# Modulation folded into the QKV weights, and tokens transposed by DMA instead of TensorE, in an attention and token-mixing kernel

## The chip, the cores and the metric

The kernel runs on one core of one Trainium2 chip. The metric is the time of one execution in microseconds (us) on the device. Each time below is a median of several executions, with the lowest and highest.

In the profiles PE is TensorE (PEld its weight loads), DVE VectorE, ACT ScalarE, POOL GpSimd, and SP the engine that issues the DMAs of the main queue.

## The reference, cut to what matters

One sequence of 2048 tokens of 512 features; 32 heads of 16 features; each token sees itself and the 255 before it.

```python
mod = (silu(c) @ w_mod).reshape(B, 6, 1, -1)
sa, ca, ga, sb, cb, gb = ...                     # shift, scale, gate; twice
h = layernorm(x) * (1 + ca) + sa                 # the modulation in question
x = x + ga * attention(h, wqkv, wo)              # softmax over a window of 256
h = layernorm(x) * (1 + cb) + sb
x = x + gb * token_mlp(h, w1, b1, w2, b2)        # gelu, products over the tokens, F = 1792
```

`sa` and `ca` are one vector each, the same for all tokens. So `h @ wqkv` equals `layernorm(x) @ ((1 + ca) * wqkv) + sa @ wqkv`: the scale can go into the rows of the weights, and the shift becomes a bias.

## The kernel before

The tokens go through in four groups (G = 0 to 3) of four tiles of 128. For each group, x is normalised (`xn`), transposed so that features lie on the partitions (`h1T`), and multiplied by the weights to give Q, K and V. Attention then runs in 75 chunks: S on TensorE (scores into PSUM), one large exp on ScalarE (`et<-psa`, about 1.45 us, and a smaller one for `psb`), and AV on TensorE. Groups 1 to 3 are projected while earlier chunks run: group 1 is needed by chunk 10 or 11, group 2 by about 30, group 3 by about 41. After the exp of the last chunk come 81.6 us, the last 66 of them mostly matmuls.

In groups 1 to 3 of the kernel before, TensorE transposes, and VectorE applies scale and shift as it copies the result out of PSUM:

```python
te.transpose(pt[:, i, tile], xn[tl][:, dc * P : (dc + 1) * P], identity[:])     # 16 a group
ve.tensor_scalar(out=h1T[:, dc, cols], in0=pt[:, i, :],                          # 4 a group
                 scalar1=modFM[:, 4 + dc : 5 + dc], scalar2=modFM[:, dc : dc + 1],
                 op0=ALU.mult, op1=ALU.add)
... # group 0 has a special first half (h1p) with the scale alone, and a Q/K bias for it
te.matmul(pq, lhsT=wqkv[:, dc, c0 : c0 + P], rhs=h1T[:, dc, cols], start=dc == 0, stop=dc == 3)
```

There is one `h1T`, so group G can be written into it only when the last projection of group G-1 has read it.

Every step is an op with a number, and the program is emitted in the order of one long list, which a search has tuned. The instructions of each engine are emitted in the order of its part of the list:

```python
def run_order(ops):
    for word in ORDER.split():            # about 1380 numbers; a letter picks the engine
        o = ops[int(word.rstrip("ADP"))]
        ...                               # error if something it depends on is not out yet
        o.emit(...)
```

The softmax here doesn't subtract the row's maximum and nothing guards it: scores larger than these inputs give would overflow.

## Time and profile before

| | kernel before |
|---|---|
| time | 267.24 us (267.21 to 267.5) |
| span of the profile | 264.8 us |
| first exp | 17.38 us |
| exp of chunk 10, 30, 41, 50, 74 | 42.45, 87.20, 111.06, 130.11, 183.23 us |
| from the exp of chunk 74 to the end | 81.57 us |
| TensorE clock | 1.00 everywhere |

### The profile page before, as it was taken

The page shows a single profiled execution, that of the slowest core. Times are in us where ns is not written, and L with a number is a line of the kernel's source. Part 1 is how long each engine was busy: PE and PEld are TensorE (multiplying, and loading weights), DVE is VectorE, ACT ScalarE, POOL GpSimd, SP SyncE. Part 2 cuts the span into 40 slices and gives each one's busy share as a digit, 9 for nine tenths or more (in the row PEclk, how much of TensorE's full clock was granted, in tenths as well). Part 3 has the DMA queues.
Part 4 walks back from the last instruction along what each step waited for, and adds up shares of the span by engine and source line. Part 5 has one row for each costly group of instructions (what it writes and reads, how often), then busy time and mean ns, then how long its engine had stood idle before and what let it go on. Part 6 is the DMA issues. An engine that isn't in the chain of part 4 may idle for free.

```text
span 264.8 us, 10695 instructions
## 1 busy us (share of the span) xinstructions
PE 248.2 (94%) x4769; PEld 136.8 (52%) x4769; DVE 193.5 (73%) x435; ACT 185.4 (70%) x268; POOL 95.9 (36%) x182
## 2 busy tenths in 40 slices
PE   7898999999998988899999999999999999999993
PEld 2576667656556654455544454445444444444441
DVE  5778896777847359999948888999998730415875
ACT  3479999999999899999999999999416431000000
POOL 8755321495289945553893031440000000000000
PEclk9999999999999999999999999999999999999999
DMA  7995400000017000000014862020499800001122
GB/s 212 369 382 197 42 5 6 2 5 2 2 49 196 5 4 5 2 2 2 5 38 128 227 172 85 2 61 23 152 362 397 360 2 0 21 0 63 59 99 79
DMA packets 31599, 25.35 MB, mean 96 GB/s; under 512 B 6076, under 2 KB 29632, under 8 KB 31552
## 3 DMA queue, kind: packets, MB, share of 16 engines
q1 hardware_dynamic: 31544, 24.66, 29.5%
q8 instruction: 37, 0.61, 0.9%
q14 instruction: 10, 0.08, 0.1%
q10 hardware_dynamic: 8, 0.00, 0.0%
HBM read 22.55 MB, written 2.10 MB: 93 GB/s over the span
## 4 chain that ended last, share of the span: by engine, by line
PE 67%; ACT 19%; DVE 8%; issue 4%; POOL 0%; ACTq 0%; POOLq 0%
PE pu L194 32%; ACT et L194 15%; PE pxy L194 13%; PE psa L194 8%; PE pq L194 5%; PE pa L194 4%; PE pv L194 3%; ACT lz L194 3%; DVE st L194 2%; DVE VT L194 1%; PE pt L194 1%; DVE part L194 1%; DVE OT L194 1%; PE psb L194 1%; DVE h L194 1%
## 5 line engine op out<-in xcount | busy, mean ns | idle before, releaser
L194 ACT ACTIVATE et<-psa 128x1536 bf16<-128x1536 f32 x75 | 109.1, 1455 | 4.0 <-PE psa L194 2.1
L194 PE MATMUL pu<-hb,w1p 128*128 128x512 bf16 x224 | 53.1, 380 | 0.8 <-DVE part L194 0.8
L194 PE MATMUL pu<-guT,w 128*128 128x512 bf16 x224 | 49.0, 379 | 0.0
L194 ACT ACTIVATE et<-psb 128x512 bf16<-128x512 f32 x75 | 45.1, 601 | 0.0
L194 PE MATMUL pxy<-et,ones_bd 128*32 128x192 bf16 (+3 forms) x960 | 38.7, 233 | 0.9 <-issue 0.9
L194 PE MATMUL pxy<-et,VT 128*32 128x192 bf16 (+3 forms) x960 | 38.4, 234 | 0.9 <-DVE OT L194 0.5
L194 PEld LDWEIGHTS <-w 128*128 128x128 bf16 x224 | 21.9, 98 | 26.4
L194 PE MATMUL psa<-QT,KT 32*128 32x192 bf16 (+3 forms) x720 | 29.8, 230 | 5.6 <-ACT et L194 4.9
L194 PEld LDWEIGHTS <-w1p 128*128 128x128 bf16 x224 | 20.3, 98 | 25.5 <-issue 2.3
L194 POOL TENSOR_SCALAR KT<-kb,mask_par 128x512 bf16<-128x512 bf16 (+1 forms) x36 | 22.9, 645 | 25.9 <-DVE kb L194 22.2
L194 PE MATMUL pq<-h1T,wqkv 128*128 128x512 bf16 (+1 forms) x128 | 30.1, 355 | 0.3 <-ACT VT L194 0.3
L194 PEld LDWEIGHTS <-KT 32*128 32x128 bf16 x960 | 16.1, 92 | 26.2 <-issue 23.9
L194 PEld LDWEIGHTS <-VT 128*32 128x32 bf16 x960 | 23.6, 96 | 11.6 <-issue 10.1
L194 PE MATMUL psb<-QT,KT 32*128 32x192 bf16 (+3 forms) x240 | 29.3, 231 | 0.0
L194 DVE SCALAR_TENSOR_TENSOR o<-pu,b2FM,bc_all 128x512 f32<-128x512 f32 x16 | 11.6, 748 | 20.2 <-PE pu L194 20.0
L194 DVE TENSOR_TENSOR et<-et,maskt 128x512 bf16<-128x512 bf16 (+2 forms) x56 | 24.9, 480 | 0.6 <-ACT et L194 0.5
L194 PEld LDWEIGHTS <-ones_bd 128*32 128x32 bf16 x960 | 23.2, 97 | 1.2 <-issue 1.1
L194 DVE BATCH_NORM_STATS2 st<-x 128x6 f32<-128x512 bf16 x32 | 21.7, 680 | 1.3 <-DMA x<-in_A_x_dram 1.1
L194 DVE TENSOR_TENSOR OT<-pxy,lz 128x256 bf16<-128x256 f32 x32 | 13.4, 420 | 10.6 <-ACT lz L194 10.1
L194 PEld LDWEIGHTS <-wqkv 128*128 128x128 bf16 x192 | 14.0, 97 | 13.4 <-issue 4.8
L194 PE MATMUL pv<-wqkv,h1T 128*32 128x256 bf16 x512 | 17.9, 274 | 0.2 <-DVE VT L194 0.2
L194 PE MATMUL pa<-wod,OT 128*128 128x512 bf16 x64 | 17.3, 381 | 0.3 <-ACT part L194 0.3
(113 smaller groups left out, 358.2 us busy)
## 6 DMA issues: line engine op xcount, KB each, us to landing
w1p<-in_B_w_dram SPq DMA_DIRECT2D x14, 512.0 KB, 6.1
w<-in_B_w_dram SPq DMA_DIRECT2D x14, 512.0 KB, 8.4
wmod<-in_w_mod_dram SPq DMA_DIRECT2D x6, 512.0 KB, 5.5
x<-in_A_x_dram SPq DMA_DIRECT2D x16, 128.0 KB, 4.8
out_dram<-otile SPq DMA_DIRECT2D x16, 128.0 KB, 1.7
wqkv<-in_A_wqkv_dram SPq DMA_DIRECT2D x2, 384.0 KB, 5.4
wqkv<-in_A_wqkv_dram SPq DMA_DIRECT2D x1, 512.0 KB, 5.0
wod<-in_A_wo_dram SPq DMA_DIRECT2D x1, 512.0 KB, 8.4
```

The costliest lines, as they stand in the source:

```text
L194: ins = call(*args, **kwargs)
```

## The change

The intent: take 48 transposes off TensorE and 12 passes off VectorE, and let the DMA queue, nearly idle at that time (DMA share 0.02 from 36 to 66 us of the kernel before), do it. The transpose in the diff takes no scale and no shift, so the modulation has to be done elsewhere: in the weights and in biases.

```diff
+# scale: rows of wqkv times (1 + ca); first heads' Q and K into a new tile wqs, the rest in place
+ve.tensor_scalar(out=dst, in0=wqkv_cols[k], scalar1=modFM[:, 4 + k : 5 + k], scalar2=0.0, ...)
+# shift: V bias by 32 narrow matmuls, copied once to SBUF
+te.matmul(ps_vb[...], lhsT=sa_rep[:, part, k, :], rhs=wv[:, k, q // 2, :, :], ...)
 # groups 1 to 3
-te.transpose(...)                                      # 16 a group
-ve.tensor_scalar(out=h1T[...], in0=pt, scalar1, scalar2, ...)   # 4 a group
+sp.dma_start_transpose(out=h1T[:, :, i * P : (i + 1) * P], in_=xn[i][:])    # 4 a group
 # Q and K leave PSUM
-ve.tensor_copy(out=QT, in_=pq)            # bias only in the first half of group 0
+ve.tensor_scalar_add(out=QT, in0=pq, scalar1=qkb)
 # V leaves PSUM
-copy(e, VT_or_vn, pv)                     # two halves of group 0 on ScalarE
+ve.tensor_tensor(out=VT_or_vn, in0=pv, in1=vb, op=ALU.add)      # VectorE alone
-xn = wpool.tile(..., bufs=5)
+xn = wpool.tile(..., bufs=4)
-ORDER = """43 3 0 4 41 ..."""
+ORDER = """44 3 0 4 31 ..."""             # searched anew, all of it
```

## The prediction

> **What bounds the kernel now.** I read the page's table of busy time first, then a cut of the execution into stretches, then the chain of work that ended last, then the groups of instructions. The table says who is full over all (columns: busy us, share of the span, instructions):
>
> ```profile
> span 264.8 us, 10695 instructions
> PE 248.2 (94%) x4769; PEld 136.8 (52%) x4769; DVE 193.5 (73%) x435; ACT 185.4 (70%) x268; POOL 95.9 (36%) x182
> ```
>
> PE leads at 94%, but that is an average over stages. The cut shows the stages (columns: stretch, its length, then busy us and count of each engine, the clock, the DMA share, GB/s):
>
> ```profile
> 17.40:36.00 18.60, 16.47 (x508) 11.98 (x500) 15.14 (x37) 17.33 (x26) 9.47 (x26) 1.00 0.52 136
> 36.00:66.00 30.00, 29.62 (x912) 19.08 (x908) 22.07 (x48) 28.52 (x37) 13.93 (x22) 1.00 0.02 4
> ...
> 76.00:123.60 47.60, 41.98 (x1192) 25.68 (x1194) 36.04 (x83) 46.43 (x62) 32.10 (x43) 1.00 0.14 36
> 123.60:154.00 30.40, 30.40 (x690) 15.95 (x687) 23.87 (x52) 29.61 (x41) 14.61 (x19) 1.00 0.39 103
> 154.00:189.00 35.00, 34.44 (x712) 17.78 (x711) 32.21 (x80) 32.89 (x52) 9.17 (x11) 1.00 0.20 54
> 189.00:199.00 10.00, 9.08 (x42) 3.92 (x41) 9.67 (x22) 2.41 (x9) 0.00 (x0) 1.00 0.97 347
> 199.00:264.80 65.80, 61.46 (x284) 27.69 (x283) 34.36 (x54) 10.59 (x16) 0.00 (x0) 1.00 0.28 106
> ```
>
> There are four kinds of time. Up to 17.4 us: a start with short dependent steps. From 17.4 to 189: attention in 75 chunks, where PE and ACT are both nearly full; ACT is idle for only 7.3 us of 171.6 (this cut with the 66 to 76 stretch included: 164.34 busy) and PE for 8.9, of which 5.6 lie in 76 to 123.6. So that middle is ACT's (46.43 of 47.60), and 36 to 76 and 123.6 to 189 are PE's with ACT 1 to 2 us behind. From 189 to 199: a DVE chain (9.67 of 10.00). From 199: matmuls alone, 284 in 61.46 us, 0.216 us each.
>
> The transposes in question, in the groups (count, busy us and mean ns, idle before) and in the chain (start, length):
>
> ```profile
> L194 PE MATMUL pt<-identity,xn 128*128 128x128 bf16 x56 | 4.1, 219 | 0.1
> L194 DVE TENSOR_SCALAR h1T<-pt,modFM 128x512 bf16<-128x512 bf16 x12 | 5.9, 535 | 0.9 <-PE pt L194 0.9
> L194 DVE CAST kb<-pq 128x512 bf16<-128x512 f32 x12 | 8.2, 682 | 1.6 <-PE pq L194 1.4
> 36.14 1.00 PE pt L194 x16
> 67.50 0.57 PE pt L194 x8
> 68.09 1.00 DVE h1T L194 x2
> 70.31 1.04 POOL rs L194
> 71.36 1.46 ACT et L194
> ```
>
> Group 1's transposes cost 1.00 us of chain, group 2's 0.45 (65.16) and 0.57, followed by 1.00 of h1T on DVE; group 3's, at 104.8, lie in ACT's stretch and are not on the chain at all.
>
> [...] a record lasts 219 ns and, pipelined, 16 took 1.00 us, 0.0625 us each[...] 128 KB here land in 1.7 us at best (the output stores), 4.8 in a busy queue[...].
>
> **The change, part by part.** The order of all instructions was laid anew, so I compared the orders of the two built programs engine by engine and priced the differences with rows of the trace.
>
> PE. 48 transposes go (64 to 16): 48 x 0.0625 = 3.0 us. The V bias adds 32 narrow matmuls of 256 columns; 64 such took 1.89 us of chain (PE pv at 17.17), so 0.95 us. Nothing else changes in count.
>
> DVE. Out: 12 h1T of 512 columns, 12 x 0.535 = 6.4 us, and 4 smaller, 1.6. In: the bias makes 24 casts of Q and K into tensor-scalar operations. With 256 columns the bias form took 477 ns (QT with qkb) against 410, so I charge 0.065 each: 1.6. V changes from cast to addition; additions from PSUM of this size run 684 (part), as the cast does (688): nothing. Two V halves come over from ACT (1.4), six weight scalings (about 2.3 by the 408 ns of an SBUF pass of 512), four multiplications or additions of h from POOL (1.7), two xn and two hb (1.7), two memsets (1.0), a vb and a sa_rep copy (0.7), a merged h1T copy (0.7). Out of DVE: four small nm (0.7). Sum: -8.0 - 0.7 + 11.1 = +2.4, spread. POOL loses about 8 us; it bounds nothing.
>
> ACT. In attention it loses two V halves and one h1T (0.59 + 0.59 + 0.57) and gains a QT and a kb of 256 columns (2 x 0.47) and one part copy (0.6): -0.2 us. So the stretch that ACT bounds hardly shortens.
>
> The start. In the kernel before, S of chunk 0 begins at 16.62 and the first exp at 17.38. In the new order DVE has the statistics of x2 and x3 ahead of modFM. x3 is issued at 4.92 and lands 4.5 us later, at 9.4; after its 0.68 and 0.18 modFM is ready at about 10.4, against 8.1 before. Behind that lie three small copies, xn x2 (0.8), the bias, h1T; on ACT two h1T of 512 (0.6 each), then two wqs (0.48 each, like h1p), then two larger scalings (1.5 together), then the first QT. I get wqs complete at 14.8, QT of the first block at 16.7, and since the two PSUM buffers of Q and K come free only then, the second block at about 17.5, S of chunk 0 near 17.8, the first exp near 18.4: +1.0 us. Against this the new order puts chunk 0 after 16 instead of 32 Q/K matmuls, so 16 of them (0.135 each, 12 took 1.62: 2.2 us) follow later.
>
> PE work from S of chunk 0 to the last output projection: 56 transposes fewer (-3.5), 16 small Q/K more (+2.2): -1.3 us. By stretches of chunks, with AV at 0.019 (64 in 1.22) and pa, pu and pq512 at 0.216: chunks 0 to 22 lose 40 transposes, 8 pa, 32 pv, 4 pq512 and gain the 16 small ones, -3.9; chunks 23 to 49 +0.8; chunks 50 to 73 gain 128 AV and 16 pv and lose 4 pu, +2.0; the rest -0.3. So work moves from the first PE-bound part into the last. In the first, ACT's idle can give back at most 3.2 us (1.27 + 1.48 + 0.44 from 17.4 to 76), of which I take 1.5. In the last, PE was full (64.84 of 65.4), so 2.0 us more cost about 1.5.
>
> The end. After the last pa both orders hold 96 + 224 matmuls: the same 69 us. The DVE chain before it has three part additions in between instead of five (-1.2 us on DVE), but PE has as much to fill the time with: 0.
>
> Sum, with the 0.2 of ACT: +1.0 - 1.5 + 1.5 - 0.3 - 0.2 = +0.5. The order was however searched for this kernel, and the pieces that I rounded (group 2's chain at 65 to 71, 2.0 us of transposes and h1T with a DVE that then runs freer) speak for some gain more; I take 1.1 for that. Net: -0.6, 267.2 to 266.6.
>
> **Rivals.** (a) The transposes by DMA come late. In group 1 all four must wait until the last Q/K of group 0 has read h1T, and the first Q of group 1 needs all four. Between these PE has 96 AV and 76 S, some 4 us of PE work, and three chunks of exp, about 6.5 us at 2.24 a chunk (74 steps in 165.85 us). [...] Groups 2 and 3 have more room (five chunks and four). For it: no trace shows such a DMA. Against: the queue is empty at 36 to 76 (share 0.02). (b) The transposes were the bound of both PE-bound parts and ACT follows: then 3.0 us go in full with the chain of group 2, giving 263. Against: ACT's few idle us. (c) The start weighs more than I think, or the weight scalings collide with the first K and Q evictions: another 1 to 2 us, 268.5. For: [...] both have the scalings ahead of the first evictions. (d) The weight loads for the later product share the queue with group 3's transposes; if they wait, group 3 starts late by a chunk, +2. The order puts only two loads ahead of them.
>
> **Range and chances.** Small terms of both signs that mostly cancel give 266.6; 264.0 if (b) holds mostly, 270.0 if (a) is moderate or (c) full. A change over 2% is 5.3 us: faster would need nearly all of ACT's idle, 0.04; slower needs a bad (a), 0.07; the rest 0.89.
>
> **What would show it.** First exp near 18.4 (start term). The exp of chunk 50 near 129 (130.11 before), ahead in spite of the later start, and that of chunk 74 about level with 183.23 (the shift of work). pt at 16 instructions, h1T on DVE gone after 40 us, kb with bias near 745 ns, vn near 690. The landing of a DMA transpose near 2 to 3 us, and no wait of PE's pq for it in groups 1 to 3. A last stretch of about 61.5 us after the hb. Wrong would be: PE idle for more than 1 us in front of pq for a DMA; a first exp before 17; an attention end earlier by over 2 us.

## More of the kernel before

Beside each execution stands the mean clock that the hardware granted to TensorE, as a share of full speed.

The starts of the exps are the ruler of this document: 75 marks that every version has, so that time lost or won can be placed between two of them. The lines of the profile that carry the reading stand in the prediction. Three rows that it doesn't show are needed later: TensorE's busy tenths in 40 slices, its granted clock in the same slices, and the shares of the chain that ended last.

```profile
PE   7898999999998988899999999999999999999993
...
PEclk9999999999999999999999999999999999999999
...
PE 67%; ACT 19%; DVE 8%; issue 4%; POOL 0%; ACTq 0%; POOLq 0%
```

The kernel before takes 267.1 to 268.0 us in all groups of runs.

## The result

The changed kernel takes 279.18 us (276.27 to 281.57, four runs) beside 267.37 us for the kernel before on the same chip: 4.05% slower. The 95% interval of the ratio is 1.0317 to 1.0493. A ratio here is the mean time of one kernel's fast runs over that of the other's in the same rounds, so it isn't quite the ratio of the medians. Executions over 1.5% slower than the fastest of the same kernel are left out of the means. One of the four runs, 281.57 us, counts as slow. The prediction of 266.6 us, with a range of 264 to 270, is wrong.

The runs of the changed kernel scatter much more than those before, and their granted clocks scatter with them: the fast runs took 276.27, 278.33 and 280.03 us at 0.988, 0.981 and 0.969. In the profiled one, (1 - 0.981) x 276.6 = 5.3 us of full-speed TensorE time are missing.

The page of the changed kernel:

```profile
span 276.6 us, 10703 instructions
...
PE 251.9 (91%) x4753; PEld 137.2 (50%) x4753; DVE 196.8 (71%) x436; ACT 185.1 (67%) x265; POOL 89.4 (32%) x178
...
PE   8699965998999798689889999999999999999993
...
PEclk9869999999999799999999999999999999999999
...
PE 57%; DVE 19%; ACT 10%; DMA 5%; issue 5%; SPq 1%; POOL 1%; DVEq 0%; ACTq 0%; POOLq 0%
```

TensorE has holes where it had none (6 in slices 2, 6 and 17, 5 in slice 7), the clock falls in slices 2, 3 and 14, and of the 19 points of the chain that PE and ACT lost, DVE and DMA have taken 16. The cut at the exps of chunks 0, 10, 30, 40 and 50 shows where the time went (columns: stretch, its length, busy us and count of PE, PEld, DVE, ACT and POOL, clock, DMA share, GB/s). Before:

```profile
0.00:17.38 17.38, 14.94 (x169) 8.55 (x173) 12.78 (x50) 8.04 (x19) 11.88 (x55) 1.00 0.95 313
17.38:42.45 25.07, 22.94 (x721) 16.69 (x710) 20.16 (x47) 23.32 (x34) 10.19 (x27) 1.00 0.39 102
...
87.20:108.95 21.75, 18.41 (x546) 11.45 (x545) 15.73 (x36) 21.62 (x30) 14.35 (x23) 1.00 0.02 4
108.95:130.11 21.16, 20.36 (x545) 12.03 (x544) 20.17 (x48) 21.14 (x29) 10.73 (x13) 1.00 0.02 4
```

After, the same chunks:

```profile
0.00:20.33 20.33, 16.64 (x183) 9.59 (x184) 13.40 (x51) 7.77 (x16) 10.66 (x53) 0.83 0.97 295
20.33:45.67 25.34, 20.70 (x644) 14.74 (x642) 19.43 (x43) 22.73 (x34) 8.32 (x16) 1.00 0.47 100
...
90.89:115.69 24.80, 21.10 (x552) 12.57 (x548) 18.97 (x43) 21.37 (x29) 15.76 (x24) 0.93 0.21 45
115.69:139.74 24.05, 19.89 (x488) 10.98 (x489) 21.01 (x50) 21.03 (x29) 6.53 (x9) 1.00 0.37 91
```

The start grew by 2.95 us at a clock of 0.83, chunks 30 to 40 by 3.05 at 0.93, chunks 40 to 50 by 2.89 at full clock. The chain of the changed kernel gives the places (start us, length, what):

```profile
3.83 4.88 DMA x<-in_A_x_dram
8.74 0.71 DVE st L193
9.65 0.59 DVE st L193
...
14.54 1.83 PE ps_vb L193 x24
16.37 1.83 PE pq L193 x8
...
43.55 3.09 DMA h1T<-xn
46.77 1.02 PE pq L193 x4
...
91.05 1.79 issue
92.84 1.77 PE pxy L193 x50
...
111.51 0.57 SPq L193
112.17 5.78 DMA h1T<-xn
118.09 1.02 PE pq L193 x4
```

- **Start.** The statistics of x2 and x3 stand ahead of modFM on VectorE, as predicted. TensorE idles from 8.58 to 10.54. After that, eight small Q/K matmuls take 1.83 us, 0.229 each; the chain before has twelve in 1.62, 0.135 each.
- **Group 1.** The first Q waits for the fourth DMA transpose until 46.64.
- **Chunk 30 to 31.** TensorE stands for 1.79 us with no wait that the profile shows ("issue"). Then 50 AV matmuls take 1.77 us, 0.035 each, where 64 took 1.22 (0.019 each) at full clock.
- **Group 3.** The fourth transpose is issued behind a weight load and takes 5.78 us.

How far each exp is behind the kernel before, in the profiles (us; the other columns are experiments, told below):

| exp of chunk | changed | e0 | e5 | e6 | s3 | b3 | b2 |
|---|---|---|---|---|---|---|---|
| 0 | 2.95 | 1.27 | 2.30 | 1.41 | 2.02 | 0.33 | 0.19 |
| 6 | 0.92 | -0.76 | 0.26 | 0.21 | -0.01 | 0.32 | 0.20 |
| 7 | 2.72 | 0.46 | 1.16 | 1.56 | 0.87 | 0.32 | 0.20 |
| 9 | 2.78 | 0.52 | 1.42 | 1.61 | 0.92 | 0.33 | 5.11 |
| 11 | 4.54 | 2.84 | 2.75 | 2.03 | 2.38 | 0.33 | 5.91 |
| 30 | 3.69 | 1.75 | 2.24 | 1.36 | 1.37 | 4.38 | 11.21 |
| 31 | 7.10 | 3.84 | 2.29 | 1.41 | 1.40 | 4.38 | 11.21 |
| 40 | 6.74 | 3.92 | 2.24 | 1.50 | 1.85 | 4.38 | 11.34 |
| 41 | 9.21 | 7.12 | 3.50 | 1.48 | 1.83 | 4.38 | 13.25 |
| 50 | 9.63 | 8.08 | 3.93 | 1.91 | 2.26 | 4.38 | 13.65 |
| 74 | 12.79 | 11.25 | 7.12 | 5.10 | 5.32 | 4.37 | 14.15 |
| end | 11.8 | 10.2 | 6.1 | 4.1 | 4.5 | 4.4 | 14.2 |

The first column read from step to step: +2.95, -2.03 by chunk 6, +1.80 to chunk 7, +0.06 to 9, +1.76 to 11, -0.85 to 30, **+3.41 to 31**, -0.36 to 40, **+2.47 to 41**, +3.58 to 74, and about -1.0 in the tail.

### The profile page after: what moved, and what is told of

Same layout as the page of the kernel before. It is cut to its first block, busy times and chain, and to the rows that moved or that the text cites.

```text
span 276.6 us, 10703 instructions
## 1 busy us (share of the span) xinstructions
PE 251.9 (91%) x4753; PEld 137.2 (50%) x4753; DVE 196.8 (71%) x436; ACT 185.1 (67%) x265; POOL 89.4 (32%) x178
## 4 chain that ended last, share of the span: by engine, by line
PE 57%; DVE 19%; ACT 10%; DMA 5%; issue 5%; SPq 1%; POOL 1%; DVEq 0%; ACTq 0%; POOLq 0%
PE pu L193 30%; PE pxy L193 9%; ACT et L193 8%; PE pq L193 6%; PE psa L193 6%; DMA h1T<-xn 3%; DVE st L193 3%; PE pa L193 2%; DVE et L193 2%; PE pv L193 2%; DMA x<-in_A_x_dram 2%; ACT lz L193 2%; DVE h L193 2%; DVE kb L193 2%; DVE part L193 1%
## 5 line engine op out<-in xcount | busy, mean ns | idle before, releaser
L193 PE MATMUL pxy<-et,VT 128*32 128x192 bf16 (+3 forms) x960 | 39.1, 236 | 3.6 <-issue 1.8
L193 POOL TENSOR_SCALAR KT<-kb,mask_par 128x512 bf16<-128x512 bf16 (+1 forms) x36 | 24.0, 678 | 32.6 <-DVE kb L193 27.4
L193 PEld LDWEIGHTS <-VT 128*32 128x32 bf16 x960 | 24.7, 97 | 14.7 <-issue 13.1
L193 PE MATMUL pq<-h1T,wqkv 128*128 128x512 bf16 (+1 forms) x120 | 25.9, 338 | 3.0 <-DMA h1T<-xn 2.5
L193 PEld LDWEIGHTS <-ones_bd 128*32 128x32 bf16 x960 | 24.0, 98 | 2.0 <-issue 2.0
L193 PE MATMUL pv<-wqkv,h1T 128*32 128x256 bf16 x512 | 18.7, 278 | 1.4 <-issue 1.4
L193 POOL TENSOR_SCALAR VT<-vn,half_m 128x512 bf16<-128x512 bf16 x24 | 17.6, 742 | 6.8 <-DVE vn L193 6.8
```

Source lines behind the costliest of these rows:

```text
L193: ins = call(*args, **kwargs)
```

## The experiments

Seventeen kernels ran in five groups; all passed the comparison with the reference. Three of them (e6, b2, b3) leave out or swap data; the comparison's tolerance didn't notice, and only their times are used. Each stands beside the kernel before in its own group. Medians and ranges are of all runs, ratios of the fast ones alone; the first group, e4 and e9 have one slow run each.

| run | us: median (range) | ratio to before, 95% interval |
|---|---|---|
| changed, first | 279.18 (276.27 to 281.57) | 1.0405 (1.0317 to 1.0493) |
| e0_control | 276.36 (275.49 to 276.93) | 1.0343 (1.0319 to 1.0368) |
| e1_start_order | 281.38 (280.27 to 281.82) | 1.0498 (1.0473 to 1.0524) |
| e2_keep_warm | 275.24 (273.62 to 276.41) | 1.0271 (1.0230 to 1.0313) |
| e3_tensor_transposes | 280.20 (278.95 to 281.80) | 1.0467 (1.0417 to 1.0516) |
| e4_queue_order | 275.39 (273.76 to 279.47) | 1.0261 (1.0221 to 1.0301) |
| e5_warm_queue | 272.75 (272.29 to 273.06) | 1.0210 (1.0193 to 1.0227) |
| e6_unread_transposes | 270.38 (270.11 to 272.02) | 1.0135 (1.0103 to 1.0167) |
| e7_tensor_early | 277.84 (277.25 to 279.01) | 1.0407 (1.0379 to 1.0435) |
| b2_dma_in_before | 278.05 (276.65 to 280.71) | 1.0399 (1.0339 to 1.0460) |
| e9_first_heads_first | 277.08 (276.49 to 280.97) | 1.0344 (1.0318 to 1.0370) |
| e10_two_buffers | 286.08 (284.77 to 286.98) | 1.0691 (1.0645 to 1.0736) |
| e11_all | 289.60 (289.43 to 291.80) | 1.0838 (1.0796 to 1.0880) |
| s1_loads_later | 275.51 (274.18 to 276.17) | 1.0306 (1.0270 to 1.0342) |
| s2_pairs | 272.14 (270.12 to 273.15) | 1.0175 (1.0118 to 1.0232) |
| s3_pairs_loads | 269.91 (269.45 to 270.99) | 1.0109 (1.0079 to 1.0138) |
| b3_free_in_before | 270.37 (268.37 to 270.91) | 1.0097 (1.0058 to 1.0135) |
| b4_spread_loads | 267.55 (267.02 to 268.36) | 0.9992 (0.9980 to 1.0003) |

In the diffs, lines with "order" show places in the list by the names of the ops.

### e1_start_order: the order of the start

```diff
-order: fm ... st(x2) fm st(x3) modFM rs(x2,x3) tr(x0,x1) nm qkb-matmuls ... wqs qkb-copy ... sa_rep
+order: fm ... fm modFM tr(x0,x1) qkb-matmuls wqs qkb-copy sa_rep st(x2) st(x3) rs(x2,x3) nm ...
```

> Changed kernel with one edit: in the start, the modulation vectors, the Q/K bias copy, the hi/lo copy for the V bias and the four scaled weight blocks of the first heads come before the statistics of token tiles 2 and 3 on VectorE and ScalarE; nothing else moves. Theory A (the order of the start is what lost it: VectorE waited for x2 and x3, TensorE stood 1.96 us and then ran at about half clock): no wait for modFM above 0.5 us, the clock digits of slices 2 and 3 at 9, the first exp at about 17.2 us instead of 20.33, the time about 3 us below the changed kernel's 279.2, so near 276. Rival B (the new bias and weight scaling work is itself too long): the first exp stays at or above 19.3 and the time within 1 us of 279.

Measured: 281.38 us, first exp 21.45, clock digits 8 and 6 in slices 2 and 3 as before the edit. Theory A fell, in the form that I gave it. The wait for modFM went, but the first Q and K still stood behind the transposes of x2 and x3 on TensorE, so the gap only moved: TensorE now idled 2.61 us, from 11.03 to 13.64, for xn of x2 and x3. Exchanging two parts of a serial chain didn't shorten it here. Rival B isn't shown either, since the gap and half clock (12.2 to 19.1 us) are in the 21.45 as well.

### e2_keep_warm: the gap filled, the waits kept

```diff
-order: fm warm fm tr(x0,x1)            # warm: one dummy matmul of 512 columns
+order: fm fm warm x9 tr(x0,x1)
```

> Changed kernel with one edit: nine more dummy matmuls of 512 columns (0.213 us each) on TensorE in the gap of 1.96 us before the second transposes, everything else in its old order, so every wait for data stays. Theory A2 (the gap itself makes the clock fall, and the fall is more than half of the 2.95 us that the first exp is late): clock digits of slices 2 and 3 at 9, vb 24 matmuls in about 0.9 instead of 1.83 us, pq 8 in about 1.1 instead of 1.83, first exp at 18.4 to 18.9, time near 277.5. Rival B2 (data waits alone): first exp stays at 20.0 or later and time near 279; also if the clock falls for another reason it still shows 8 and 6.

Measured: 275.24 us, ratio 1.0271 against 1.0405 and 1.0343 of the two groups of the changed kernel. First exp 19.21, a little above what was expected, and by chunk 5 it was level with the kernel before (+0.03 us). The clock in the two kernels over the same 6.9 us, the changed kernel first, with its stretch after the stall at chunk 30 as well:

```profile
11.40:18.30 6.90, 6.81 (x81) 4.43 (x78) 4.38 (x16) 3.06 (x7) 3.67 (x16) 0.51 1.11 347
...
92.84:98.00 5.16, 5.16 (x125) 3.61 (x125) 1.50 (x5) 2.47 (x4) 1.65 (x4) 0.67 0.02 6
```

```profile
11.40:18.30 6.90, 5.88 (x95) 4.13 (x96) 6.00 (x22) 4.29 (x9) 3.62 (x16) 1.00 1.10 344
```

Half clock (0.51) against full clock (1.00): work that does nothing, put into the gap, kept the clock up in this profile and made the kernel faster. That part of theory A2 holds. Its other part holds too. x3 landed 0.87 us later in this profile than in the first, so the first exps don't compare directly; from modFM (ready at 10.56 and 11.42 us) to the first exp it took 9.77 us in the changed kernel and 7.79 in e2. The fall cost about 2.0 of the 2.95 us. Some of the gain in time lies elsewhere, since chunk 30 to 31 took 2.15 us in this profile instead of 5.51.

### e0_control: the changed kernel once more

> The changed kernel itself once more, as the control of this group of runs on one chip. All theories: 276 to 282 us, mean granted clock between 0.96 and 0.99, first exp near 20.3. If the clock drops sit at the same places as in its first profile (11 to 18 us and 91 to 97 us), they belong to the order of the work; if they move from run to run, they depend on how the gaps fall in time.

Measured: 276.36 us, in another group of runs. The first exp came at 18.65 in this profile and the start had full clock; the clock now fell from 41.1 to 44.5 and from 116.2 to 119.6 us instead. So the places of the drops aren't fixed by the order of the work. A plain pair for it: TensorE waits 1.57 us for ScalarE ahead of chunk 9's scores in the first profile of the changed kernel (40.95 to 42.51) and in e3 (39.39 to 40.96). In the first, full speed followed (clock 1.00 from 42.10 to 45.52); in e3, half clock (0.50 from 41.23 to 44.64). And in s1 (below), a gap of 2.58 us (112.31 to 114.89) was followed by full clock.

The traces show what the drops have in common. Each drop to half clock lasts 3.41 us or twice that, and within one trace the drops start whole multiples of 3.41 us apart: 11.38 and 93.31 in the changed kernel are 24 apart. So I cut each of the 14 fast profiles with a drop into windows on its own grid. Ahead of all 22 drops, TensorE had been idle for at least 1.77 us of the window just before. Of the 1046 windows at full clock that no drop followed, two had that much (1.80 in e0, 1.88 in s1). The wait of 1.57 us is an example. In e3 all of it lies in one window, which idles 3.41 - 1.51 = 1.90 us in sum, and the next runs at half clock. In the changed kernel it falls into two, the first of which idles 1.49. First e3, then the changed kernel:

```profile
37.82:41.23 3.41, 1.51 (x76) 1.19 (x78) 1.11 (x4) 3.41 (x6) 0.00 (x0) 1.00 0.00 0
41.23:44.64 3.41, 3.22 (x94) 2.87 (x84) 2.00 (x4) 2.36 (x4) 0.00 (x0) 0.50 0.02 5
```

```profile
38.69:42.10 3.41, 1.92 (x74) 1.28 (x65) 1.74 (x5) 3.20 (x4) 0.00 (x0) 1.00 0.31 44
42.10:45.52 3.42, 2.31 (x112) 2.07 (x111) 2.60 (x6) 3.40 (x7) 0.00 (x0) 1.00 0.70 118
```

So the length of a single gap doesn't tell: gaps of 1.57 us (e3) and 1.96 us (changed kernel) were followed by half clock, and one of 2.58 us (s1) wasn't. The sum over a window of the grid tells more, with at least 1.77 us ahead of all 22 drops. The grid doesn't begin with the execution: the drops at 11.38 us in the first profile of the changed kernel and at 41.1 us in e0, the same kernel, are 8.7 times 3.41 us apart. That fits drops that move from run to run with the work unchanged.

### e3_tensor_transposes and e7_tensor_early: the DMA transposes undone

```diff
-sp.dma_start_transpose(out=h1T[:, :, i * P : (i + 1) * P], in_=xn[i][:])   # 4 a group
+te.transpose(pt[...], xn[tl][...], identity[:])                           # 16 a group
+ve.tensor_copy(out=h1T[:, dc, :], in_=pt[:, j, :])                         # 4 a group
 order e3: all of a group just ahead of its first projection
 order e7: in two halves, earlier; with the edits of e2, and group 3's xn early as in e4
```

> Changed kernel with the 12 DMA transposes of groups 1 to 3 undone: 48 TensorE transposes and 12 plain VectorE copies instead, each group's placed behind the AV work that stands just before its first projection; weights and biases as changed. Theory A3 (the DMA transposes lose 1.3 us in group 1 and 2.5 in group 3, partly because they wait in the queue, more than the 3 us of TensorE work that they save where TensorE is not the bound): time 2 to 4 us below 279.2, so 275 to 277; chunk 10 to 11 takes 2.3 us instead of 3.44, chunk 40 to 41 at most 2.9 instead of 4.58. Rival B3 (they are hidden and the loss is elsewhere): the time goes up by 1 to 3 us, since TensorE and VectorE take the work back. If the two cancel, within 1 us.

> The same kernel as e5_warm_queue with the transposes of groups 1 to 3 on TensorE and 12 plain VectorE copies, now placed better than in e3: group 1's first half in the 1.57 us in which TensorE waits for ScalarE before chunk 9's scores, the second half behind these scores, groups 2 and 3 also in two halves. Theory (four DMA transposes in a row, 1.2 us or more each in the queue and 2.4 to 3 to land, are slower than 1 us of TensorE and 1.5 of copies): 1 to 2.5 us below e5_warm_queue, chunk 10 to 11 at most 2.4 us. Rival (TensorE has no room for 3 us more): equal or up to 2 us above.

Measured: 280.20 us for e3 and 277.84 for e7, which is 5.1 us above e5 in the same group. Both theories fell: undoing the part that looked guilty gained nothing. The ratio of e3 lies above that of e0 in another group, and not clearly above that of the first group. In e3, TensorE waited 0.85 us between the two halves for the copies in group 1, and again in group 3. In e7, chunk 10 to 11 took 2.10 us, as hoped, but chunks 9 to 10, 25 to 27 and 39 to 40 lost it again. In both, the queue no longer waited for transposes, so four weight loads went out together around 85 to 93 us, and TensorE's stall there grew to 2.15 and 1.99 us. The order was searched for DMA transposes; that its loads, evictions and PSUM buffers fit no other is likely and not shown. So these two runs don't say that TensorE transposes are bad; they say that putting them back into this order, in these two places, lost.

### e4_queue_order: the last transpose ahead of the loads

```diff
-order: xn2 hb touch w1p-load touch hb hb xn3 ... transpose3    # group 3; GpSimd and the queue
+order: xn2 xn3 transpose3 hb touch w1p-load touch hb hb
```

> Changed kernel with one edit: the fourth normalised tile and the fourth DMA transpose of group 3 stand before two hb, two small copies and a 512 KB weight load on GpSimd and the DMA queue, instead of behind them. Theory A4 (the transpose was issued late and landed in 5.78 us because a weight load was in front of it): it lands in 2.4 to 3.2 us, the first Q of group 3 no longer waits for a DMA by more than 0.5 us, chunk 40 to 41 takes about 2.3 to 2.6 us instead of 4.58, time about 2 us lower, near 277. Rival B4 (a transpose is slow by itself, whatever is in the queue): landing stays above 4 us and the time within 0.7 us of 279.2.

Measured: 275.39 us. Chunk 40 to 41 took 3.31 us instead of 4.58, and TensorE's waits for transposes summed to 2.7 us (4.1 in the first profile of the changed kernel, 3.8 in e0). The longest landing was 4.2 us. The direction of A4 holds; a rest of 1.2 us stayed. The other weight loads start right behind the fourth transpose; that they cause the rest isn't shown. The fast runs of e4 span 273.76 us at clock 1.000 to 276.02 at 0.987, so its gain in time isn't this step alone.

### e5_warm_queue: both together

The edits of e2 and e4.

> Changed kernel with both edits of the runs before: nine dummy matmuls in the gap of the start, and the fourth transpose of group 3 ahead of hb, small copies and weight load. Theory: the losses are separate terms, so what stays over the kernel before is group 1's wait for its transposes (1.5), the late VectorE at chunk 7 (0.7), a rest of group 3 (1.2) and the work moved behind chunk 41 (2.6), about 6: 273 to 274, clock 0.99 to 1.00 and fewer differences between runs. Rival (both runs won the same 3 to 4 us, because both happened to miss the clock drop at 91 us): 275 to 276.

Measured: 272.75 us, 273 to 274 expected; clock 0.991 to 1.000, and a range of only 0.8 us. It is 5.65 us above the kernel before, where e0 in the same group is 9.26 above it and the first group 11.81: four tenths to half of the loss is gone with nothing done to the arithmetic. The rival's figure, 275 to 276, is out.

### e6_unread_transposes: nobody waits for the DMA

```diff
-rhs=h1T[:, dc, cols]
+rhs=h1T[:, dc, cols] if G == 0 else xres[4 * G + dc][:]      # wrong on purpose; V likewise
```

> The same kernel as e5_warm_queue, wrong on purpose: the projections of groups 1 to 3 read tiles of x instead of h1T, so the 12 DMA transposes still run and nothing waits for them. Theory: the wait for them is worth group 1's 1.5 us and group 3's 1.2 us: about 2.5 us below e5_warm_queue, no wait of pq for a DMA. Rival (another wait, of VectorE or ScalarE, ends at about the same time): less than 1 us below.

Measured: 270.38 us, 2.37 below e5 in the same group, as expected (2.5). TensorE's waits list for e5 has this line (us, times, longest), and e6's list has none for a DMA:

```profile
PE pq L193 <- DMA h1T<-xn: 1.6, 2, 1.2
```

So in the mended order the waits for the transposes are worth 2.4 us, with what follows from them: the profile of e5 has one clock drop of 3.41 us, that of e6 none. Even with free transposes and nearly full clock (0.99 to 1.00), the changed kernel stays 1.35% behind. The e6 column says where: chunk 6 to 7 (+1.35), and chunk 50 to 74 (+3.19, with about 1.0 back in the tail).

### e9_first_heads_first, e10_two_buffers, e11_all: three attempts that lost

```diff
 e9: order: ... modFM tr(x0,x1) qkb-matmuls wqs K0 Q0 evictions, then st, xn, tr of x2 and x3   (+ e4)
 e10:
-h1T = wpool.tile([P, ND, D], BF, name="h1T"); E_BUFS = 6
+h1Ts = [wpool.tile([P, ND, D], BF, name=f"h1T{n}") for n in range(2)]; E_BUFS = 5
 order e10: xn and transposes of groups 1 and 3 earlier                                        (+ e5)
 run_order e10: a number waits in the list until what it depends on is out, instead of an error
 e11: e9 and e10, without the dummies of e2
```

> Changed kernel with the queue edit of e4 and another order of the start: the first K and Q, which need only x0 and x1, on TensorE ahead of the transposes of x2 and x3, with their weight blocks, bias and evictions ahead of the statistics of x2 and x3; no added dummy matmuls. Theory (the serial chain x2, x3, modFM, then all Q/K is what makes the start late): no gap above 1 us, first exp at 16.5 to 17.5, chunk 5 about 1 to 1.5 us earlier than in e5_warm_queue, time 271 to 272. Rival (the exps of chunks 1 to 7 wait for other Q/K and V work anyway): chunk 7 within 0.5 us of e5_warm_queue and time 272.3 to 273.

> e5_warm_queue with two h1T buffers instead of one (paid for with 5 instead of 6 exp tiles), and the normalised tiles and DMA transposes of groups 1 and 3 issued earlier, which a second buffer allows. Theory (the wait for the transposes comes from the single h1T, which lets the first of them start only behind the last projection of the group before, with some 5.7 us left for four in a row): no wait of pq for a DMA above 0.3 us, time near the 270.4 of e6_unread_transposes, so 270 to 271. Rival (five exp tiles hold back ScalarE, or VectorE gets later elsewhere): 272.5 or more.

> Both edits together: first heads first in the start, two h1T buffers with early transposes, and the queue edit. Theory (separate terms): the sum of what the two runs gain over e5_warm_queue, so 268.5 to 270, still 1.5 to 3 us above the kernel before, because the added VectorE work and the work moved behind chunk 41 stay. Rival (one hides the other): no better than the better of the two by more than 0.3 us.

Measured: 277.08, 286.08 and 289.60 us. e9: its fast runs, 276.49 to 277.42, are no better than e4's (273.76 to 276.02), and the theory of the start isn't supported. e10 removed the wait for the DMA entirely, but lost far more elsewhere. TensorE's waits in e5 and in e10, and a wait of ScalarE in e10 that e5's list doesn't have:

```profile
PE psa L193 <- ACT et L193: 5.3, 16, 1.6
```

```profile
PE psa L194 <- ACT et L194: 19.4, 31, 1.8
...
ACT et L194 <- PE pxy L194: 16.7, 17, 2.0
```

The last line is exps that wait, 17 times, for AV matmuls to have read an exp tile: the price of five tiles instead of six. As a test of the second buffer the run is spoilt by this price, and what a second `h1T` alone would give is open, since no run has it beside six exp tiles. e11, with both edits, lost most.

### b2_dma_in_before: the DMA transposes alone, in the old order

```diff
 # kernel before
+            if G:
+                sp.dma_start_transpose(out=h1T[:, :, i * P : (i + 1) * P], in_=xn[i][:])
-            16 TensorE transposes and 4 VectorE passes a group        # wrong on purpose: no modulation
```

> The kernel before with one part of the change alone: groups 1 to 3 transposed by 12 DMAs, each issued right behind its normalised tile, in the old order of everything else; wrong on purpose, since these groups are then not modulated. 48 TensorE transposes (3.0 us) and 12 VectorE passes (6.4 us) go. Theory (in a row of four the DMAs land too late: first issue after the last projection of the group before, 1.2 to 1.3 us each in the queue, 2.4 to 3 us for the last): the first pq of group 1 waits some 3 to 4 us, groups 2 and 3 together 0 to 3, some of it given back, time 268.5 to 272. Rival (as predicted, they fit and the transposes' TensorE time is gained): 265 to 267.

Measured: 278.05 us, worse than either theory. Group 1 cost 5.72 us from chunk 8 to 11 (in the old order its first projection comes only about 4 us after the last of group 0): TensorE waited 3.34 us for the transposes, and the clock was half from 40.2 to 47.0. Group 3 cost 1.91 us. Another 4 us went from chunk 28 to 30, where TensorE stood for 2.70 us without a visible wait and then ran slow. In this profile half clock covers 20.5 us in all, three drops of 6.83. So this one part of the change, put into the old order, loses as much as the whole change in its own, the clock included.

### b3_free_in_before: the same with nobody waiting

b2 with the projections of groups 1 to 3 reading tiles of x, as in e6: the DMA transposes run, TensorE and VectorE are relieved, nothing waits.

> The kernel before, wrong on purpose: the 12 DMA transposes run as in b2 and the 48 TensorE transposes and 12 VectorE passes are gone, but the projections of groups 1 to 3 read tiles of x, so nothing waits for a transpose. Theory (the prediction's premise: work taken off TensorE and VectorE is worth 1 to 3 us in this order, if only nothing waits): 264.8 to 266.8. Rival (the removed work stood beside ScalarE's exps and gives nothing, or the weight loads now issued later bring a stall as in b2): 267.3 or more, and a stall near chunk 28.

Measured: 270.37 us. The kernel before and b3, from the exp of chunk 0 to that of chunk 28:

```profile
17.38:82.13 64.75, 61.51 (x1883) 40.63 (x1874) 47.98 (x106) 61.53 (x83) 33.67 (x62) 1.00 0.23 59
```

```profile
17.71:82.46 64.75, 58.70 (x1841) 38.88 (x1843) 44.23 (x98) 61.52 (x84) 33.67 (x62) 1.00 0.32 75
```

TensorE has 2.8 us and VectorE 3.7 us less to do, and the stretch takes 64.75 us in both. From chunk 30 to 74 the distance stays at 4.38 or 4.37 as well. **The removed work was worth nothing in this order, even free.** The exps follow each other at the same pace; ScalarE is busy for 61.5 of the 64.75 us in both. The new order says much the same: in e6, from chunk 0 to 22, the distance goes from 1.41 to 1.53 us with free transposes. What b3 loses is one event between chunks 28 and 29, with half clock for 3.41 us behind it (in brackets what the idle time ahead is put down to):

```profile
86.56 2.11 PE L194 MATMUL pv<-wqkv,x 128*32 128x256 bf16 x35 [3.62 <-issue]
```

### s1_loads_later: the stall at chunk 30

```diff
-order: ... w1p-load w1p-load (near chunk 28) ... five w1p-loads (behind group 3)
+order: ... five w1p-loads, w1p-load w1p-load (all behind group 3)
```

> Changed kernel with one edit: the first two 512 KB loads for the later product, issued near chunk 28, stand behind the other five of their kind, after group 3's transposes. Theory (the loads make TensorE's stall at chunk 30 to 31, for example by holding up its instructions): no issue stall above 0.9 us there, chunk 30 to 31 at most 2.8 us instead of 5.5 and 4.2 in the two profiles of the changed kernel, time 2 to 3 us below 276.4 to 279.2, so 274 to 276.5. Rival (the stall belongs to the place in the program): a stall of at least 1.2 us at the same matmuls, time as the changed kernel.

Measured: the stall is gone. Chunk 30 to 31 in the changed kernel, and in s1:

```profile
90.89:96.40 5.51, 3.72 (x109) 3.04 (x106) 3.01 (x8) 2.32 (x3) 3.41 (x6) 0.72 0.02 4
```

```profile
90.63:92.76 2.13, 2.13 (x109) 1.84 (x102) 2.10 (x6) 2.13 (x3) 1.93 (x4) 1.00 0.05 12
```

The same 109 matmuls take 2.13 us instead of 5.51. In time the gain is less clear (275.51 us; ratio 1.0306, its interval overlaps that of e0), and the clock of its four runs is 0.975 to 0.988: in the profiled one it fell from 41.4 to 48.2 us instead.

Which mechanism? The DMA view lists a queue `q8 instruction`, with 37 packets in the whole profile of the changed kernel. One of them lies in the quarter of a microsecond from 90.25, at the very end of the two weight loads:

```profile
q8 instruction: 1, 0.02, 29.4%
```

TensorE resumes at 92.84, 2.3 to 2.6 us later. In e0, such a packet comes from 88.25 and TensorE resumes at 90.91; in e3 94.25 and 97.09; in b2 89.25 and 92.18; in b3 83.75 and 86.56; in the kernel before 83.50 and 86.16. In s1, without the loads, packets lie near 87.25 and 91.0 and there is no stall. So TensorE resumes 2.3 to 2.9 us after a packet that came late, behind the weight loads. That the loads make the stall is shown by s1; that instructions arrive late is argued from these times, for the profile doesn't name the engine that a packet is for. In the changed kernel 6.7 us lie between this packet and the one before it, where 3.5 to 5 are usual; in the kernel before, the packet isn't late by that measure.

### s2_pairs and s3_pairs_loads: half as many transposes

```diff
-h1T = wpool.tile([P, ND, D]);     4 x sp.dma_start_transpose(out=h1T[:, :, i * P : (i + 1) * P], in_=xn[i])
+h1T = wpool.tile([P, 4, ND, P]);  2 x sp.dma_start_transpose(out=h1T[:, i - 1 : i + 1], in_=xn_pair)
 s2: with e5's edits; s3: with e5's and s1's
```

> e5_warm_queue with two tiles to one DMA transpose, so 6 issues instead of 12; h1T laid out by tile for it. Theory (the row of issues at 1.2 us each is what is late): the second transpose of group 1 has landed at least 1.2 us earlier after the last projection of group 0, the waits of pq for a DMA fall from 1.6 to below 0.7 us, time 0.7 to 1.5 us below 272.75. Rival (a transpose of twice the size takes twice the time to issue or land): issue near 2.4 us or landing above 4.5, waits and time as e5_warm_queue or worse.

> s2_pairs with the loads moved as in s1. e5_warm_queue had a stall of only 0.7 us at chunk 30 to 31, so the theory of the loads expects 0.3 to 0.8 us less than s2_pairs, about 271; rival: no difference within 0.3 us, or slower if the late loads arrive late for the product.

The transposes of the changed kernel, then of s2 (issue time ns as lowest/median/highest, first and last start; then the time from issue to landing):

```profile
L193 SPq DMA_TRANSPOSE h1T<-xn x12: 1188/1215/2545, 38.2 to 112.2; - x12
...
DMA to landing us min/median/max: 2.4/2.9/5.8
```

```profile
L193 SPq DMA_TRANSPOSE h1T<-xn x6: 1233/1260/1505, 37.0 to 107.2; - x6
...
DMA to landing us min/median/max: 3.1/3.2/3.4
```

Two tiles cost one issue of 1.26 us and land in 3.2 us: the issue hardly grows, and the landing by 0.3 to 0.6 (2.9 in the changed kernel, 2.6 in e5). All waits of pq for a DMA vanished. s2 took 272.14 us, 0.6 below e5's median but not clearly (it ran in another group, and its runs scatter from 270.12 to 273.15). Chunk 40 to 41 takes 2.09 us, and s2 still had the stall, 1.35 us. s3 without it: 269.91 us, the best changed version, 1.1% behind the kernel before. Its gain over s2, 2.2 us, is larger than the 0.3 to 0.8 expected, but the intervals of the two ratios overlap. The stall of s2 is longer than the 0.7 us that the expectation took from e5; the mean clock of both is 0.993. The rest isn't explained.

### b4_spread_loads: is the stall worth something before?

```diff
-order: three w1p-loads together at chunk 25
+order: one there, one behind chunk 31's scores, one behind chunk 40's
```

> The kernel before with one edit: of the three 512 KB weight loads that it issues together at 76.89 us, one stays, one goes behind chunk 31's scores and one behind chunk 40's. Theory (instruction packets wait behind loads): no issue stall above 0.3 us at chunk 29 to 30, which takes 2.2 us instead of 2.93, time 0.5 to 0.9 us below the kernel before, so about 266.4 to 266.8. Rival (ScalarE's exps have the slack to hide 0.9 us there): within 0.2 us of the kernel before.

Measured: 267.55 us, ratio 0.9992 (0.9980 to 1.0003): the same. The one stall of 0.87 us became three, of 0.28, 0.43 and 0.33 us, and from the exp of chunk 10 to that of chunk 50 it took 88.07 us, where the kernel before takes 87.66. The rival's figure holds. No version that ran beats the kernel before.

## Why the prediction was wrong

**The gain had no place to go.** The prediction credited the removed PE work with 1.5 us in chunks 0 to 22 ("In the first, ACT's idle can give back at most 3.2 us", of which it took 1.5), and 1.1 more, mainly for group 2. This step failed. b3 measures it in the old order: 0.00 us, with the work gone and nothing to wait for. In the new order, with free transposes (e6), the distance from the kernel before grows by 0.12 us from chunk 0 to 22 instead of falling by 1.5. A PE row of 8 and 9 in nearly every slice, and an ACT that idles now and then, didn't mean that less PE work lets ACT start earlier.

**Rival (a) was right in a mild form, 1.6 us of waiting in group 1, and my sum against it was wrong.** The sum put the four landings below the 6.5 us of three chunks of exp; the landing times in it were my estimate, and no run had shown them. The four transposes of group 1 took 8.4 us in the changed kernel, from 38.24, right behind the last projection of group 0, to 46.64. Four landings of the median 2.9 us would make 11.6 one after the other, so they overlap and weren't the term: each transpose holds the queue for 1.2 us (the first even 2.54), and the last then needs 3.09. Group 3 had room, but a weight load and GpSimd's order in front, rival (d), which I had named with 2 us and not taken into the sum; it was 2.47. The waits of both groups: 4.1 us as delivered, and 2.4 us of time even in the mended order (e5 to e6).

**Two things were missing from the sum.** The first is the clock. Every row of the profile before reads 1.00, and I priced each step at that rate. The change opened gaps in TensorE, and TensorE came back at half speed: 0.51 for 6.9 us of the start, 0.67 for 5 us behind the stall. The predicted first exp, 18.4, is about what the changed kernel does when the clock holds (18.65 in e0, 18.58 in s1); in the first profile it was 20.33, though modFM was ready at 10.56 us, near the 10.4 predicted. So "+1.0 us" at the start was sound as a sum of steps (+1.27 measured), and it costs nothing in the end, since e0 is 0.76 us ahead by chunk 6. The second is TensorE's stall behind the weight loads. The kernel before has it too, 0.87 us, and there its split into three smaller ones left the time the same (b4, ratio 0.9992). In the new order it was 1.8 us, with a clock drop behind it in one profile: +3.41 and +2.09 us.

**What was right.** The shift of PE work into the last part was priced at +1.5 us with 0 for the end; measured from chunk 50 to 74 +3.16, tail about -1.0, together +2.1. The count of 128 more AV matmuls there was right (704 against 580 before by the trace: 124), and the tail gave a part back, which I hadn't counted. The bias form of V was free, as said; the changed kernel's group line has 687 ns, the cast before 688:

```profile
L193 DVE TENSOR_TENSOR vn<-pv,vb 128x512 bf16<-128x512 f32 x12 | 8.2, 687 | 4.9 <-PE pv L193 4.9
```

The landing (median 2.9 us) lay in the expected 2 to 3. The sign "no wait of PE's pq for it in groups 1 to 3" was wrong: 4.1 us in two waits.

**What stays open.** Chunk 6 to 7, +0.7 to +1.8 us in all fast profiles of the new order: TensorE stands 0.5 to 1.4 us in front of some of group 0's last V matmuls, without a visible wait, while VectorE, alone with all V evictions, is late. No run separates the two. The other half of the change, the modulation in weights and biases, was never run alone, so its own cost isn't known. For the clock, windows with 1.77 to 1.88 us of idle time went both ways, and why some drops last twice 3.41 us isn't settled. The gains of the mends don't simply add up to the loss, since the mean clock changes with them as well (0.969 to 0.988 in the fast runs of the changed kernel, 0.991 to 1.000 in e5, 0.975 to 0.988 in s1).

## What to carry to other kernels

Before pricing work taken off a full engine, ask what paces it: here the removed TensorE and VectorE work stood beside exps that went on at their own pace (64.75 us for chunks 0 to 28 with it and without it, b3), and was worth nothing even when it was free. A transfer put in place of an instruction has to be priced as a row: issues in one queue, what else is in that queue, and how late the first may start, not landings alone. Here the transpose of one 128 KB tile held the issuing queue for 1.2 us at the median, where the plain 512 KB loads of w1p took 0.48, and landed in 2.9 us, where the plain 128 KB stores landed in 1.7. A block of 128 columns cost 0.73 us of landing that way, a quarter of 2.9, and 0.0625 us in a row of 16 TensorE transposes that took 1.00 us. Bursts of loads belong in the price too: stalls of TensorE of up to 3.62 us (b3) came behind two to four loads of 512 KB, and the one of 1.79 us in the changed kernel went away with its loads (s1). And an order tuned to one set of operations holds gaps, loads and buffers that fit that set; new idle gaps on TensorE cost more than their length here (behind the one of 1.96 us at the start the clock was 0.51 for 6.9 us), so look at the granted clock first: it fell after windows of 3.41 us in which TensorE's idle time summed to about 1.8 us.
